# Seven SBUF buffers in one ring for output tiles, transposed w3 tiles and the remainders' gate products

## The chip, the core and the metric

The kernel runs on one core of one Trainium2 chip. The metric is the device time of one execution in microseconds. Before the change the median of three runs is 421.14 us (419.65 to 421.98). The engines are named as in the profile: PE is TensorE, with PEld for its weight loads, DVE is VectorE, ACT is ScalarE, POOL is GpSimd, and SP is SyncE, which here only issues transfers (DMAs).

## What is computed

An attention over 8 batches of 8 heads, whose queries are averaged in pairs, and then a feed-forward part with a product in place of an activation:

```
q_pool = q.reshape(B, H, S // 2, 2, D).mean(axis=3)          # 8, 8, 576, 64
attn = softmax(q_pool @ k.transpose / sqrt(D))               # keys: 1152
x = (attn @ v).transpose(0, 2, 1, 3).reshape(B * 576, H * D) # 4608 x 512
out = ((x @ w1) * (x @ w2) @ w3) @ w_out                     # w1, w2: 512 x 1024
```

Here w3 is 1024 x 1024 and w_out 1024 x 512. Output and inputs are float32; the kernel works in float16 with sums in float32.

## The kernel before

**Attention.** The heads are taken in 32 pairs P. POOL issues the loads of k, q and v (L110, L118, L125). The first pairs are transposed on PE, the later ones by transposing DMAs on SP (kT at L168, qT at L174). Scores are made in chunks of 512 columns for two heads (L296), in a PSUM tile `psc`; ACT takes the exponential into the ring `er` (L302). When a pair's scores are done, `attend` multiplies them with v (L315, L324) in bursts: 36 matmuls for each head into a PSUM bank `po`, plus 18 for the last 64 columns. DVE divides by the sums (L348, L351) and SP transposes the result into `xT` (L356). The last 64 of the 576 queries of a head, the remainders, go into `rems` (L362) and by transposes of their own (L335) into `xR`, which is copied across halves on DVE (L377).

**Feed-forward.** w3 @ w_out is multiplied once into `T16`: `w3_transpose` transposes a block of w3 on PE (L486), DVE copies it in two halves into a tile `w3T` (L477), and PE multiplies it with w_out (L498). For each batch, `gate` makes x @ w1 and x @ w2 into one PSUM bank (`pg`, L539). A copy of the first half goes to `asb` (DVE at L518; in the tail ACT at L515), and DVE multiplies both into the gate product `gT` (L531). `rows` multiplies `gT` with `T16` into a PSUM tile `pp` (L563). `store` evicts it, scaled, into a tile `osb` of 128 x 512 float32 (DVE at L553; in the tail ACT at L549), and `store_rows` has SP store that to the output (L629). The last tile is evicted in halves by `last_rows` (L640 on ACT, L643 on DVE; stores at L647).

The remainders of four batches form a unit of their own (`split=True`), once in the middle and once at the end. Its gate products are two tiles of 128 x 8 x 128 float16; they live until the unit's output rows are multiplied.

**Order.** The program is written out in Python with a manual schedule. A planner keeps one clock for each half of PE's rows (`clock`), times of DVE and of ACT, and two queues for each half: `prep` (transposes) and `ffn` (feed-forward blocks). It emits a chunk of scores when ACT will take it, a burst of `attend` when a pair is done, and otherwise the next feed-forward product (`step`). A block takes one of four PSUM banks with `take` and gives it back when its eviction is planned to end (`give`). So the order on each engine is fixed when the program is built; on the chip, each engine works its list in order, and semaphores hold an instruction until its operands and its buffer are there. `seen` and the loads of a pair five ahead follow each kT.

**Buffers.** A tile of the pool `ffp` has a tag; tiles of one tag share `bufs` buffers in turn. When a tile gets a buffer, its first writer waits for the last readers of the tile that had it. For an `osb` tile the last reader is its store. The tags that matter are `osb` with three buffers, and `w3T` with four, which the remainders' `gT` use too. All of these tiles have 2048 bytes in a partition. `w3T` tiles are written from 23.8 to 54.7 us, and no more than four of them are alive, which the planner takes care of (`len(w3T) < 4` at L765).

Of the kernel before, what the change touches and what calls it, by code (L numbers as in the profile page):

```python
# [7 lines left out]
FP32 = mybir.dt.float32  # L8
FP16 = mybir.dt.float16
# [14 lines left out]
def kernel(  # L24
# [13 lines left out]
    dm = H * D  # L38
# [3 lines left out]
    NF = dff // 128  # L42
# [9 lines left out]
    ffp = ctx.enter_context(tc.tile_pool(name="ffp", bufs=2))  # L52
# [33 lines left out]
    def vector(n, at):  # L86

        nonlocal vec
        vec = max(vec, at + T_SEM) + 0.16 + n / 960
        return vec  # L90

    def bank(pre, n, dt=FP32):
        if n >= 4:
            return psum.tile([128, 2, 512], FP32, tag="psc", bufs=2, name=pre)[:, 0, :]
        return psum.tile([128, 2048 // (4 if dt == FP32 else 2)], dt, tag=f"ff{n}", bufs=1,
                         name=pre)

    def take():
        return spare.pop(0)[1]
# [330 lines left out]
    w3T = {}  # L430
# [31 lines left out]
    def add(queue, block, cost, ready, emit):  # L462


        for h in block.tiles:
            for n in range(block.n_products):
                queue[h].append((block, n, cost, ready(n) if callable(ready) else ready, emit))

    def w3_transpose(c):

        w3T[c] = ffp.tile([128, NF, 128], FP16, tag="w3T", bufs=4, name="w3T")
        ready = [1e9]
        left = [2]
        landed = 13.0

        def out(t, at, h):
            nc.vector.tensor_copy(out=w3T[c][:, :, 64 * h:64 * h + 64],  # L477
                                  in_=t[:, 0:512].rearrange("p (a f) -> p a f", f=64))
            done = vector(256, at)
            left[0] -= 1  # L480
            if left[0] == 0:
                ready[0] = max(done + T_SEM, landed)
            return done

        def emit(t, s, n, start, stop):
            nc.tensor.transpose(t[:, 64 * n:64 * n + 64],  # L486
                                w3h[c // 2][s, c % 2, 128 * n:128 * n + 128], ident[s, s])
        for h in range(2):
            add(prep, Block("w3t", NF, (h,), lambda t, at, h=h: out(t, at, h), FP16),
                0.0285, [[0.0]], emit)  # L490

        def copy(t, at):
            nc.vector.tensor_copy(out=T16[:, c, :], in_=t)
            del w3T[c]
            return vector(512, at)

        def product(t, s, n, start, stop):
            nc.tensor.matmul(t, w3T[c][s, n, :], wosb[s, n, :], start=start, stop=stop,  # L498
                             skip_group_check=True)
        add(ffn, Block("pT", NF, (0, 1), copy), 0.216, [ready], product)  # L500

    def unit(x, places, ready, split=False, final=False):

        gT = {}
        gdone = [[[1e9] for _ in range(NF)] for _ in range(2)]
        n = 256

        def gate(ft, h):  # L510
            def mul(t, at):
                asb = ffp.tile([128, n], FP32, tag="asb", bufs=3, name="asb")
                b, a = t[:, n:2 * n], asb
                if tail:
                    nc.scalar.copy(out=a, in_=t[:, 0:n])  # L515
                    at += 0.4
                else:
                    nc.vector.tensor_copy(out=a, in_=t[:, 0:n])  # L518
                    vector(n, at)
                if h not in gT:  # L520
                    if split:
                        g = ffp.tile([128, NF, 128], FP16, tag="w3T", bufs=4, name="gT")
                        gT[h] = g.rearrange("p a f -> p (a f)").rearrange(
                            "p (a f) -> p a f", f=n)
                    else:
                        gT[h] = ffp.tile([128, NF, n], FP16, tag="g", bufs=4, name="gT")
                g = gT[h][:, ft % 4 if split else ft, 0:n]
                if not split:
                    g = g.rearrange("f (i p c) -> f i c p", p=64, c=2)
                    b, a = (y.rearrange("f (i c p) -> f i c p", c=2, p=64) for y in (b, a))  # L530
                nc.vector.tensor_mul(out=g, in0=b, in1=a)  # L531
                done = vector(n, at)
                gdone[h][ft][0] = done + T_SEM
                return done
            fs = slice(ft * 128, ft * 128 + 128)

            def emit(t, s, i, start, stop):
                w, m = divmod(i, H)
                nc.tensor.matmul(t[:, n * w:n * w + n], (w1sb, w2sb)[w][s, (m + h) % 2, m // 2, fs],  # L539
                                 x(h, s, m),  # L540
                                 start=start, stop=stop, skip_group_check=True)
            add(ffn, Block("pg", 2 * H, (h,), mul), 0.0025 + n / 2400,
                [ready, copied[2 * ft // NF]], emit)

        def rows(h, o, places):
            def store(t, at):
                osb = ffp.tile([128, dm], FP32, tag="osb", bufs=3, name="osb")
                if tail:
                    nc.scalar.activation(out=osb, in_=t, func=AF.Copy, bias=0.0,  # L549
                                         scale=1.0 / (SCL * SCL))  # L550
                    done = at + T_SEM + 0.65
                else:
                    nc.vector.tensor_scalar_mul(out=osb, in0=t, scalar1=1.0 / (SCL * SCL))  # L553
                    done = vector(512, at)
                store_rows(osb, places)
                return done
            cs = slice(o, o + 128)

            def g(s, i):
                return gT[i // 4][s, i % 4, cs] if split else gT[h][s, i, cs]  # L560

            def emit(t, s, i, start, stop):
                nc.tensor.matmul(t, g(s, i), T16[s, i, :], start=start, stop=stop,  # L563
                                 skip_group_check=True)
            if final:
                last.append((emit, store, places, lambda i: g(slice(0, 128), i)))
            else:
                add(ffn, Block("pp", NF, (0, 1), store), 0.216,
                    lambda i: [gdone[i // 4 if split else h][i]], emit)

        yield gate
        for h, o, to in places:
            rows(h, o, to)
# [43 lines left out]
    def rows_out(places, cols):  # L617

        (b0, c0), (b1, c1) = places
        if b0 == b1:  # L620
            rows = out[b0 * SQ:(b0 + 1) * SQ, cols].rearrange("(p c) m -> p c m", c=NJ)
            return [(slice(0, 128), rows[:, c0:c0 + 2])]
        return [(slice(64 * s, 64 * s + 64),
                 out[b * SQ:(b + 1) * SQ, cols].rearrange("(p c) m -> c p m", c=NJ)[c])
                for s, (b, c) in enumerate(places)]

    def store_rows(osb, places):
        for r, rows in rows_out(places, slice(0, dm)):
            nc.sync.dma_start(out=rows, in_=osb[r])  # L629

    def last_rows(places, lhsT):
        osb = ffp.tile([128, dm], FP32, tag="osb", bufs=3, name="osb")
        for h in range(2):
            hs = slice(256 * h, 256 * h + 256)
            pp = bank("pp", take())
            for ft in range(NF):
                nc.tensor.matmul(pp[:, hs], lhsT(ft), T16[:, ft, hs],  # L637
                                 start=(ft == 0), stop=(ft == NF - 1))
            if h == 0:
                nc.scalar.activation(out=osb[:, hs], in_=pp[:, hs], func=AF.Copy, bias=0.0,  # L640
                                     scale=1.0 / (SCL * SCL))
            else:
                nc.vector.tensor_scalar_mul(out=osb[:, hs], in0=pp[:, hs],  # L643
                                            scalar1=1.0 / (SCL * SCL))
            for s, (r, rows) in enumerate(rows_out(places, hs)):
                eng = nc.sync if s == 0 else nc.scalar
                eng.dma_start(out=rows, in_=osb[r, hs])  # L647
# [56 lines left out]
    c = 0  # L704
# [65 lines left out]
    for emit, store, _, _ in last[:-1]:  # L770
        n = take()
        t = bank("pp", n)
        for i in range(NF):
            emit(t, slice(0, 128), i, i == 0, i == NF - 1)
        give(n, store(t, clock[0]))
    last_rows(*last[-1][2:])


# [28 lines left out]
```

## Time and profile before

| what | us |
|---|---|
| median of three runs | 421.14 |
| the profiled execution | 418.11 |
| its span, from the first to the last instruction | 416.2 |
| evictions of `pp` by DVE (L553) | 26 of 0.69, from 118.9 to 347.3 |
| evictions by ACT (L549) | 9 of 0.60, from 375.8 to 410.7 |
| stores of `osb` by SP (L629) | 38, from 122.6 to 411.9 |
| a store from issue to landing, whole tiles | 4.0 (median) |

The granted TensorE clock was 1.00 throughout. One execution is profiled; its own time is its span and 1.9 us around it. A line of the profile's groups of instructions names the source line, the engine, the operation, what is written from what (`osb<-pp`), its count and its time. `[3.00 <-DMA x]` behind a line of the timeline is idle time of the engine before that instruction, and what ended it. An engine with the letter q (SPq) stands for issuing or waiting, not for work. The chain of work that ended last is followed back from the last instruction, at each step to what released it.

### The profile page before, as it was taken

What the parts mean: (1) busy time and instruction counts of PE and PEld (TensorE: products, weight loads), DVE (VectorE), ACT (ScalarE), POOL (GpSimd) and SP (SyncE); (2) the same over time, 40 slices, a digit from 0 to 9 for tenths busy, and PEclk for the clock granted to TensorE, in tenths of its full rate; (3) what the DMA queues carried; (4) which work ended last, traced back from release to release, by engine and by line L of the source; (5) the groups of instructions that cost most, each with busy time, mean ns of one, the idle gap of its engine ahead of it and who ended that gap; (6) DMA issues with size and microseconds to landing.
All of it is one profiled execution on the core that took longest, in us unless ns stands there. A gap on an engine that the chain in (4) does not pass through costs nothing.

```text
span 416.2 us, 16886 instructions
## 1 busy us (share of the span) xinstructions
PE 398.7 (96%) x7410; PEld 315.5 (76%) x7410; DVE 219.0 (53%) x586; ACT 323.5 (78%) x368; POOL 191.5 (46%) x209
## 2 busy tenths in 40 slices
PE   3699999999999999999999999899999999999996
PEld 1376775868769987987789886797789878987873
DVE  3256668765536644654466644365456645653530
ACT  3978889989889888778888987888887887854432
POOL 8244334870666676645656575566676400000000
PEclk9999999999999999999999999999999999999999
DMA  8999999999999998999999999999995155102004
GB/s 128 200 206 203 180 189 192 191 173 162 140 149 160 196 149 141 195 146 113 195 185 143 135 146 180 200 161 143 138 179 94 27 84 138 23 19 106 2 17 138
DMA packets 94217, 58.98 MB, mean 142 GB/s; under 512 B 64832, under 2 KB 84544, under 8 KB 94144
## 3 DMA queue, kind: packets, MB, share of 16 engines
q0 software_dynamic: 26528, 33.56, 53.1%
q1 hardware_dynamic: 67456, 24.22, 36.5%
q8 instruction: 58, 0.95, 1.0%
q10 hardware_dynamic: 160, 0.13, 0.1%
q14 instruction: 15, 0.12, 0.1%
HBM read 67.11 MB, written 9.44 MB: 184 GB/s over the span
## 4 chain that ended last, share of the span: by engine, by line
PE 91%; ACT 4%; DMA 2%; issue 1%; DVE 1%; POOL 0%; DVEq 0%; POOLq 0%
PE pg L539 29%; PE psc L296 19%; PE po L315 18%; PE pp L563 15%; PE pT L498 4%; ACT er L302 4%; PE po L324 3%; DMA out_dram<-osb 1%; PE t L264 1%; DMA kst<-in_k_dram 1%; PE sw L412 1%; PE w3t L486 1%; PE pp L637 0%; DVE osb L553 0%; PE tb L197 0%
## 5 line engine op out<-in xcount | busy, mean ns | idle before, releaser
L302 ACT ACTIVATE er<-psc 128x1024 f16<-128x1024 f32 x324 | 303.6, 1038 | 54.9 <-PE psc L296 54.8
L296 PE MATMUL psc<-qT,kT 64*128 64x512 f16 (+7 forms) x1152 | 130.0, 291 | 4.3 <-ACT er L302 3.9
L539 PE MATMUL pg<-xT,w2sb 64*128 64x256 f16 x1024 | 120.7, 269 | 0.1
L539 PE MATMUL pg<-xT,w1sb 64*128 64x256 f16 x1024 | 118.9, 269 | 1.0 <-issue 1.0
L539 PEld LDWEIGHTS <-w1sb 64*128 64x128 f16 x1152 | 90.4, 94 | 9.1 <-issue 1.3
L539 PEld LDWEIGHTS <-w2sb 64*128 64x128 f16 x1152 | 91.0, 94 | 6.4 <-issue 0.2
L563 PE MATMUL pp<-T,gT 64*128 64x512 f16 (+1 forms) x552 | 92.7, 376 | 0.0
L296 PEld LDWEIGHTS <-kT 64*128 64x128 f16 x1152 | 62.5, 95 | 31.6 <-issue 16.6
L315 PEld LDWEIGHTS <-er 128*128 128x128 f16 x2304 | 73.9, 98 | 13.5 <-issue 11.7
L315 PE MATMUL po<-vt,er 128*128 128x65 f16 x2304 | 80.3, 194 | 1.2 <-DVE osb L553 1.1
L531 DVE TENSOR_TENSOR gT<-pg,asb 128x256 f16<-128x256 f32 x144 | 64.2, 446 | 17.9 <-ACT asb L515 12.8
L518 DVE COPY asb<-pg 128x256 f32<-128x256 f32 x117 | 49.1, 420 | 34.5 <-PE pg L539 34.2
L348 DVE RECIPROCAL rz<-po 128x4 f32<-128x4 f32 x64 | 12.1, 189 | 82.0 <-PE po L315 43.7
L145 POOL TENSOR_TENSOR qp<-qst 64x1152 f16<-64x1152 f16 x23 | 54.5, 2368 | 1.0
L563 PEld LDWEIGHTS <-gT 64*128 64x128 f16 (+1 forms) x552 | 37.8, 94 | 17.2 <-issue 0.4
L170 POOL COPY seen<-kT 1x1 f16<-1x1 f16 x19 | 3.4, 181 | 80.9 <-DMA kT<-kc 80.9
L154 POOL COPY vt<-vst 128x1152 f16<-128x1152 f16 x28 | 32.1, 1150 | 3.9 <-issue 2.9
L125 POOL DMA_DIRECT2D vst<-in_v_dram x32 | 23.2, 725 | 17.1 <-DMA kst<-in_k_dram 6.1
L118 POOL DMA_DIRECT2D kst<-in_k_dram x33 | 24.0, 728 | 11.7 <-issue 3.0
L163 POOL COPY kc<-kst 128x1152 f16<-128x1152 f16 x23 | 26.8, 1163 | 5.7 <-DMA kT<-kc 5.7
L351 DVE TENSOR_TENSOR xn<-po,rz 128x256 f16<-128x256 f32 x64 | 27.2, 424 | 2.2
L498 PE MATMUL pT<-wosb,w3T 64*128 64x512 f16 x128 | 26.2, 377 | 0.0
(66 smaller groups left out, 238.1 us busy)
## 6 DMA issues: line engine op xcount, KB each, us to landing
qst<-in_q_dram POOLq DMA_DIRECT2D x32, 288.0 KB, 7.4
vst<-in_v_dram POOLq DMA_DIRECT2D x32, 288.0 KB, 9.0
kst<-in_k_dram POOLq DMA_DIRECT2D x31, 288.0 KB, 6.0
out_dram<-osb SPq DMA_DIRECT2D x32, 256.0 KB, 4.0
w3h<-in_moe_w_dram POOLq DMA_DIRECT2D x4, 512.0 KB, 15.2
wosb<-in_moe_w_out_dram POOLq DMA_DIRECT2D x1, 1024.0 KB, 13.7
xT<-xn SPq DMA_TRANSPOSE x64, 5.9
w1sb<-in_moe_w_dram POOLq DMA_DIRECT2D x2, 512.0 KB, 15.8
```

What stands on the lines that cost most here:

```text
L145: (eng or nc.vector).tensor_tensor(out=qps[pp][r].rearrange("p c u d -> p u c d"), in0=src[:, :, :, 0, :], in1=src[:, :, :, 1, :], op=ALU.add)
L154: (eng or nc.vector).tensor_copy(out=vts[P % 4][:, :, :, 0:D], in_=vst.pop(P))
L163: nc.gpsimd.tensor_copy(out=kc.rearrange("p j u d -> p u j d"), in_=kst.pop(P))
L296: nc.tensor.matmul(t[:, u, o:o + ln], kT[P][s, j, :], qv[s, f0:f0 + ln], start=True, stop=True)
L302: nc.scalar.activation(out=er[:, :, r:r + CH], in_=psc.pop(c), func=AF.Exp, bias=0.0, scale=SCALE)
L315: nc.tensor.matmul(po[:, VW * i:VW * i + D + 1], er[:, u, r:r + 128], vts[P % 4][:, u, j, 0:D + 1], start=(j == 0 and i == 0), stop=(j == ...
L351: nc.vector.tensor_tensor(out=xn, in0=acc[:, 0:4, 0:D], in1=rz[:, 0:4].to_broadcast([128, 4, D]), op=ALU.mult)
L498: nc.tensor.matmul(t, w3T[c][s, n, :], wosb[s, n, :], start=start, stop=stop, skip_group_check=True)
L518: nc.vector.tensor_copy(out=a, in_=t[:, 0:n])
L531: nc.vector.tensor_mul(out=g, in0=b, in1=a)
L539: nc.tensor.matmul(t[:, n * w:n * w + n], (w1sb, w2sb)[w][s, (m + h) % 2, m // 2, fs], x(h, s, m), start=start, stop=stop, skip_group_chec ...
L563: nc.tensor.matmul(t, g(s, i), T16[s, i, :], start=start, stop=stop, skip_group_check=True)
```

## The change

Two tags become one. The w3 tiles, the remainders' gate products and the output tiles share one ring of seven buffers, as many bytes as before:

```diff
     def w3_transpose(c):
-        w3T[c] = ffp.tile([128, NF, 128], FP16, tag="w3T", bufs=4, name="w3T")
+        w3T[c] = ffp.tile([128, NF, 128], FP16, tag="row", bufs=7, name="w3T")
...
                     if split:
-                        g = ffp.tile([128, NF, 128], FP16, tag="w3T", bufs=4, name="gT")
+                        g = ffp.tile([128, NF, 128], FP16, tag="row", bufs=7, name="gT")
...
             def store(t, at):
-                osb = ffp.tile([128, dm], FP32, tag="osb", bufs=3, name="osb")
+                osb = ffp.tile([128, dm], FP32, tag="row", bufs=7, name="osb")
...
     def last_rows(places, lhsT):
-        osb = ffp.tile([128, dm], FP32, tag="osb", bufs=3, name="osb")
+        osb = ffp.tile([128, dm], FP32, tag="row", bufs=7, name="osb")
```

The other gate products keep their own tag with four buffers. The planner's clocks, costs and limits are the same, and so is every call that emits an instruction.

## The prediction

> **What bounds the kernel now.** I read the page from the top: its first part for the engines, its fourth for the chain that ended last.
>
> ```profile
> span 416.2 us, 16886 instructions
> ...
> PE 398.7 (96%) x7410; PEld 315.5 (76%) x7410; DVE 219.0 (53%) x586; ACT 323.5 (78%) x368; POOL 191.5 (46%) x209
> ...
> PE 91%; ACT 4%; DMA 2%; issue 1%; DVE 1%; POOL 0%; DVEq 0%; POOLq 0%
> ```
>
> PE is busy for 96% of the span and holds 91% of the chain. So a changed wait on DVE, ACT or SP counts only as far as it makes PE pause. The same line of the chain has 2% for DMA; the chain by line puts 1% on `out_dram<-osb`, a store of an output tile. That does not belong on a chain in the middle of a kernel, so I asked for the waits around that tile.
>
> ```profile
> its engine sat idle before it (us, times) until:
>   PE pp L563: 17.8, 26
>   PE pp L637: 6.2, 2
>   DMA out_dram<-osb: 3.0, 1
> who waited for it (us, times):
>   DVE osb L553: 3.0, 1
>   PE po L315: 1.1, 1
> ...
> DMA to landing us min/median/max: 2.0/4.0/8.0
> ```
>
> Of all the evictions into osb tiles exactly one, with 3.0 us of idle time, waited for a store (for a buffer); the others waited for PE's product. One wait of PE, 1.1 us, was in turn for that eviction. The timeline of that stretch, first SP, then DVE, then PE:
>
> ```profile
> 259.07 3.60 SPq L356 DMA_TRANSPOSE xT<-xn  x2
> 262.76 1.18 SPq L335 DMA_TRANSPOSE wosb<-rems  x1
> 264.04 1.21 SPq L629 DMA_DIRECT2D out_dram<-osb  x2
> ```
> ```profile
> 259.32 0.69 DVE L553 TENSOR_SCALAR osb<-pp 128x512 f32<-128x512 f32 x1 [0.19 <-PE pp L563]
> ...
> 265.89 0.45 DVE L531 TENSOR_TENSOR gT<-pg,asb 128x256 f16<-128x256 f32 x1
> 269.34 0.69 DVE L553 TENSOR_SCALAR osb<-pp 128x512 f32<-128x512 f32 x1 [3.00 <-DMA out_dram<-osb]
> ```
> ```profile
> 267.72 1.27 PE L315 MATMUL po<-vt,er 128*128 128x65 f16 x36
> 270.08 1.25 PE L315 MATMUL po<-vt,er 128*128 128x65 f16 x36 [1.09 <-DVE osb L553]
> ```
>
> The tile written at 259.32 is full at 260.01. Its store is issued only at 264.04, since SP works in order and first issues three transposes (3.60 and 1.18 us). The store lands at 264.04 + 5.21 = 269.25 (5.21 is its piece in the chain). Three tiles later the ring of three is round: DVE is free at 265.89 + 0.45 = 266.34, the product was ready before that (DVE's wait for PE that the eviction carries ended at 265.83 by the semaphore's record), and it sits until 269.34. Its eviction frees the PSUM bank that the second half of an attention burst wants, so PE pauses 1.09 us.
>
> **The change, step by step.** I laid the instruction listings of the two programs side by side. On PE, DVE, ACT, POOL and SP every instruction, DMA issues included, stands in the same place; nothing is added, removed or moved. The planner's own rule (at most four w3T at once) is untouched. What differs is buffer addresses and the waits of DVE and ACT for a buffer. So the work is to take each eviction, find the new previous holder of its buffer, and read from the trace of before when that holder was done.
>
> 1. The one wait that goes. The osb tile at 269.34 no longer waits for the store issued at 264.04; in the new ring its buffer was last read by a store that landed at 259.44, and the product is ready at 265.83. So it starts behind the gate product at 266.36 or so, 3.0 us earlier, and ends at 267.05. Next late for PE is then nothing of this eviction: the second 36 matmuls of the burst can follow the first 36, which end at 268.99. PE saves 270.08 - 268.99 = **1.09 us**; the other 1.9 us of the wait were hidden under PE's gate matmuls and the first half of the burst.
>
> 2. The other 25 evictions on DVE and the 11 by ACT and DVE at the end (9 of L549, one each of L640 and L643). Before, all were ended by PE, so dropping waits for landed stores gains nothing. The tightest of these was the tile at 263.69, whose store had landed at 263.21, 0.48 us earlier. In the new ring the smallest margin between a buffer's release and its use is 5.0 us (the last tile: released 406.58, used 411.56). In the places where the new listing has a store's wait, it ended long ago.
>
> 3. Waits that are new. Two gate products of the last remainder batch (L531 at 394.78 and 397.06) now also wait for stores, of tiles that landed at 349.33 and 352.81: over 44 us early, cost nothing. If they were late, ACT's asb copies and the PE gate banks behind them would be, at up to the whole delay. The two copies to asb at 382.15 and 382.69 name an ACT instruction 8 us and more earlier: nothing. The w3T evictions (L477) keep exactly their waits. A queue instruction for an extra wait takes 21 ns on DVE (L553 has 19 of them, median 21 ns); a few go and come, none while PE waits: nothing, and bounded by 19 x 0.021 = 0.4 us either way.
>
> 4. Different addresses. No row shows an instruction whose time hangs on its buffer: the 26 evictions into three buffers take 676 to 693 ns. I take zero; the bound, were all 26 at the other end of that spread, is 0.4 us off the path.
>
> Does 1.09 us reach the end? Behind 270 the list of PE's waits has only this pause and one of 1.0 us for nothing that the profile shows; the stage from 272 to 363 has PE busy 90.02 of 91.00 us, and ACT, busy 76.13 there, has idle time in front of it at every burst to move along (3.19 us before 272.17, where the burst before had 2.01). DVE's copy of the remainders at 293.84 has the smallest margin to a transfer behind 270, 0.45 us. If that transfer did not come earlier too, DVE would wait 0.6 us; DVE's 3.0 us wait above showed that some 1.9 us can be hidden there, and I take the price as zero. The tail ends with matmuls and fixed stores and moves along.
>
> Sum, on the profiled execution (418.11 us, of which 416.2 span and 1.9 around it): 418.11 - 1.09 = 417.0. The median of the runs shown is 421.14, 3.0 above the profiled execution; no row says where those 3.0 go, and I leave them in both kernels: 421.14 - 1.1 = **420.0**.
>
> The trace's store took 5.21 us. The Trainium skill, DMA: Bandwidth & Descriptors, section Anatomy of one DMA, fits 2.0 us plus the bytes by 436 GB/s (it measured transfers issued by GpSimd; this one is SP's). For 256 KB that is an estimate of 2.6 us, the wait would be 0.3 us, PE would not pause, and the change would give nothing: that is the first rival below. This trace does not agree, with a median of 4.0 us; the measurement decides.
>
> **The rivals.**
>
> *No gain.* DVE's wait costs PE only what goes beyond 1.9 us, so the store has to land later than 264.04 + 4.1. This one took 5.2; the median of all is 4.0, the shortest 2.0. In an execution where it takes the median, PE does not pause even before the change, and the time stays 421.1. Against it: the stretch 264 to 272 moves 250 GB/s, the most of six stretches that I compared (157 in the long one before it, 109 behind), because a pair's loads of k, q and v (3 x 288 KB) are issued at 259.07 to 261.1, and they belong to the program, not to chance.
>
> *A larger gain.* The timed runs are 1.5 to 3.9 us longer than the profiled execution. If part of this is stores that land later, the old ring pays and the new one does not. At the largest landing time seen, 8.0 instead of 5.2, the pause is 1.1 + 2.8 = 3.9 us, and the time 417.2. The tile at 263.69, with a margin of 0.48, would be late too. For it: four evictions before the tail had margins of 0.5 to 2.1 us. Against it: in this profile all but one were met.
>
> *Slower: PE's instructions arrive late.* PE paused twice with no wait that the profile shows, 0.56 us before 180.91 (L324) and 0.98 us before 282.47 (L539). I read them as a late block of instructions: queue q8 brings 58 packets, 0.95 MB, some 16 KB each. The change moves all of PE behind 270 by 1.1 us against the transfers, so other blocks can be late. At 0.98 us each, one more cancels the gain; four more make 420.0 + 3.9 = 423.9. The point from which it is slower by 0.5% is (2.1 + 1.1) / 0.98 = 3.3 blocks. Against it: 2 of 58 were late in the whole span, and there are only some 25 behind 270. The Trainium skill, Runtime: NRT & Kernel Launch, section Instruction fetch mechanics, says that the fetch is mostly hidden; the two pauses are the exception here, if my reading of them is right.
>
> *The change doesn't do what it says.* If the pool handed out buffers so that a tile waits for a gate product still in use, time would be lost; the listing shows no such wait.
>
> **How the numbers follow.** Forecast, about 1 us off (0.3 to 2.1): 0.52, at 420.0. No gain, within 0.3 us or a little over: 0.15, at 421.1. Larger gain, over 2.1 us: 0.23, at 417.2. Slower rival: 0.10, at 423.9. That the change doesn't do what it says: under 0.01, and left out. The runs before spread 419.65 to 421.98, so under 0.5% (2.1 us) a measurement of this kernel can hardly be told from no change. Faster by over 0.5% is the larger gain, 0.23; slower by over 0.5% needs three to four late blocks, 0.08, and one or two of them leave it within; the rest, 0.69, is within 0.5%. The range goes from 417.4, just short of the largest store, to 421.9, where a median without gain could fall within the runs' spread (421.1 + 0.8); about 0.2 lies outside.
>
> **What would show it.** In the profile after, the waits around osb should have no row for `out_dram<-osb`; PE po L315 should have no wait for DVE osb L553; a burst of 72 should stand whole (2.3 us) near 267.7, and ACT's idle time at the next exponential fall from 3.19 to about 2.0. PE's busy time stays near 398.7 and the span falls to about 415.1. What would prove me wrong: a new wait of DVE or ACT for a store, more pauses of PE by "issue" (rival three), or timed runs that fall by far more than the one pause of the profile (rival two).

## The result, and the profile after

| | median us | runs |
|---|---|---|
| before, measured with the change | 420.23 (417.94 to 423.20) | 16 |
| after | 417.94 (414.81 to 419.83) | 16 |
| ratio after to before | 0.9951, 95% interval 0.9928 to 0.9973 | |

The change makes the kernel faster by 0.49%, which is 2.1 us of 420.2; the interval goes from 1.1 to 3.0 us. The forecast was 1.1 us, and 420.0 for a median that now measures 417.9, inside the range but near its lower end. Of the 2.1 us between these two, 0.9 is the median of before, which is 421.14 over three runs and 420.23 over 16; the rest is the gain.

The page of the kernel after:

```profile
span 416.9 us, 16877 instructions
...
PE 398.7 (96%) x7410; PEld 315.2 (76%) x7410; DVE 220.1 (53%) x586; ACT 323.6 (78%) x368; POOL 191.4 (46%) x209
...
PE 92%; ACT 4%; issue 1%; DMA 1%; DVE 1%; POOL 0%; DVEq 0%; POOLq 0%
```

PE is as busy as before to the tenth. DMA fell from 2% of the chain to 1%. Yet this span is not shorter but 0.7 us longer than the one of before; experiment 9 comes back to it. The waits around the output tiles in the kernel after:

```profile
its engine sat idle before it (us, times) until:
  PE pp L563: 17.4, 25
  PE pp L637: 6.2, 2
who waited for it (us, times):
```

The row for `out_dram<-osb` is gone, and nobody waits for an eviction. Then the place of the old pause, SP, DVE and PE of the kernel after:

```profile
263.66 1.19 SPq L335 DMA_TRANSPOSE wosb<-rems  x1
264.95 1.21 SPq L629 DMA_DIRECT2D out_dram<-osb  x2
```
```profile
265.77 0.45 DVE L531 TENSOR_TENSOR gT<-pg,asb 128x256 f16<-128x256 f32 x1
266.11 0.68 DVE L553 TENSOR_SCALAR osb<-pp 128x512 f32<-128x512 f32 x1
```
```profile
267.60 2.37 PE L315 MATMUL po<-vt,er 128*128 128x65 f16 x72
```

The tile that stood until 269.34 is evicted right behind the gate product, and the burst of 72 matmuls is whole. The store that it used to wait for is still late: issued at 264.95, and by its semaphore it landed at 271.73, 6.8 us later (5.2 in the first profile of before). By this landing, a ring of three would have held DVE some 2.5 us longer here than in the first profile of before.

### The profile page after: what moved, and what is told of

Read it like the earlier page. It is cut to its first block, busy times and chain, and to the rows that moved or that the text cites. A ratio compares the mean times of both kernels' runs of the same rounds, so it can differ in the third digit from the quotient of the medians.

```text
span 416.9 us, 16877 instructions
## 1 busy us (share of the span) xinstructions
PE 398.7 (96%) x7410; PEld 315.2 (76%) x7410; DVE 220.1 (53%) x586; ACT 323.6 (78%) x368; POOL 191.4 (46%) x209
## 4 chain that ended last, share of the span: by engine, by line
PE 92%; ACT 4%; issue 1%; DMA 1%; DVE 1%; POOL 0%; DVEq 0%; POOLq 0%
PE pg L539 29%; PE psc L296 18%; PE po L315 18%; PE pp L563 15%; PE pT L498 4%; ACT er L302 4%; PE po L324 3%; DMA kst<-in_k_dram 1%; PE t L264 1%; PE sw L412 1%; PE w3t L486 1%; PE pp L637 0%; DVE wosb L377 0%; PE tb L197 0%; POOL qst L110 0%
```

## The experiments

**Theory A**: the gain is the one wait of output tile 17 (counted from 0; the eviction at 269.34) for the store of tile 14; in most executions this store lands later than in the first profile, and so the pause is larger than 1.1 us. **Theory B**: several evictions wait for stores in the timed runs, and the gain is spread over them. **Theory C**: the new addresses matter, not the wait. Two more rivals, D and E, come up below.

### 1. One tile alone gets another buffer

```diff
-                osb = ffp.tile([128, dm], FP32, tag="osb", bufs=3, name="osb")
+                n, made[0] = made[0], made[0] + 1
+                if n == 17:
+                    osb = ffp.tile([128, dm], FP32, tag="w3T", bufs=4, name="osb")
+                else:
+                    osb = ffp.tile([128, dm], FP32, tag="osb", bufs=3, name="osb")
```

> The kernel before, in which the one output tile that waited (number 17 counted from 0, written at 269.3 us) takes a buffer of the ring of four w3 tiles, and nothing else is changed. Theory A, that the whole gain is this one wait: the same ratio to before as the changed kernel, 0.995 (0.993 to 0.997), and no eviction waits for a store around 266. Theory B, that the gain is spread over several evictions that only in the timed runs wait for a store (the tile at 263.7 had a margin of 0.5 us): less than half of it, 0.998 to 1.000. Theory C, that the new addresses matter and not the wait: 1.000.

Ratio to before 0.9955 (0.9931 to 0.9979). One tile of 36 in another buffer gives the gain of the whole change, which is theory A's figure. The profile also holds a wait at a later tile, which the first profile of before does not have; first that eviction on DVE, then the burst on PE:

```profile
310.46 0.69 DVE L557 TENSOR_SCALAR osb<-pp 128x512 f32<-128x512 f32 x1 [1.40 <-DMA out_dram<-osb]
```
```profile
268.67 2.37 PE L315 MATMUL po<-vt,er 128*128 128x65 f16 x72
```

At 310.46 tile 21 waits 1.40 us for a store, and no wait of PE follows from it: a wait under 1.9 us was hidden here too.

### 2. All tiles but that one

The same two branches, with the condition

```diff
-                if n == 17:
+                if n < 12 or 18 <= n < 30:
```

> The complement: tiles 0 to 11 and 18 to 29 take buffers of the ring of four, tiles 12 to 17 and the last ones keep the ring of three, so that the wait of tile 17 for the store of tile 14 stays, while nearly all other tiles have more room. Theory A: ratio 1.000 to before (0.998 to 1.002), DVE waits 3 to 6 us for a store at tile 17, and PE pauses 1 to 4 us there. Theory B: at least half of the gain, 0.997 or less.

Ratio 1.0003 (0.9978 to 1.0028): with that wait in place, more room for the others gives nothing. DVE, then PE:

```profile
270.55 0.69 DVE L557 TENSOR_SCALAR osb<-pp 128x512 f32<-128x512 f32 x1 [4.07 <-DMA out_dram<-osb]
```
```profile
267.85 1.27 PE L315 MATMUL po<-vt,er 128*128 128x65 f16 x36
271.29 1.25 PE L315 MATMUL po<-vt,er 128*128 128x65 f16 x36 [2.17 <-DVE osb L557]
```

DVE waits 4.07 us and PE pauses 2.17: the 1.9 us between the two are what PE had to do meanwhile, as in the first profile (3.00 and 1.09).

### 3 and 4. A ring of five, a ring of six

The changed kernel with another count in all four places:

```diff
-tag="row", bufs=7
+tag="row", bufs=5
```

> The changed kernel with a ring of five in place of seven. Two of the five hold the remainders' gate products while tiles 12 to 17 are written, which leaves three: by the listing, tile 17 waits for the store of tile 14 again. Theory A: ratio 1.000 to before, the pause of PE is back (1 to 4 us), though the addresses are again others and the other tiles have rings of five. Theory B: about 0.997. Theory C gives no reason why five should differ from seven: 0.995.

> The changed kernel with a ring of six. Tile 17 then waits for the store of tile 13, which landed at 263.2 in the profile of before, 2.6 us before it is needed (262.2 in the one after). Theory A: 0.995, as with seven, no wait for a store. If the stores of the timed runs are so late that even tile 13's is late (over 2.6 us later than in the profile), 0.997.

Five: 0.9992 (0.9964 to 1.0021). Six: 0.9944 (0.9918 to 0.9971). With five the wait is back; DVE, then PE of the ring of five:

```profile
269.83 0.69 DVE L553 TENSOR_SCALAR osb<-pp 128x512 f32<-128x512 f32 x1 [4.30 <-DMA out_dram<-osb]
```
```profile
270.58 1.43 PE L315 MATMUL po<-vt,er 128*128 128x65 f16 x36 [2.40 <-DVE osb L553]
```

The burst of the ring of six:

```profile
268.92 2.37 PE L315 MATMUL po<-vt,er 128*128 128x65 f16 x72
```

With six no eviction waits for a store, and the gain is there. So it is a threshold, in the number of buffers left while two hold the remainders' gate products: three are one too few, four are enough. The interval of the ring of five reaches down to theory B's 0.997, so there it is the pause in its profile that speaks for theory A. Theory C falls, since all rings from five to seven have new addresses, and with five the gain is gone. The ring of six costs 2048 bytes per partition less than the change, at the same time within the intervals.

### 5. The store that is late, issued by another engine

The kernel before, ring of three. One store of 38 goes out from ACT, so that it does not stand in SP's queue:

```diff
-                store_rows(osb, places)
+                store_rows(osb, places, nc.scalar if n == 14 else nc.sync)
```

> The kernel before with its ring of three, in which the store of tile 14 alone is issued by ACT and not by SP, so that it does not stand behind the transposes in SP's queue (4.0 us between the tile's end and the issue in the profile of before). Theory A, with the queue as the reason why the store is late: issued near 260.5 it lands near 265 to 266, tile 17 does not wait (or under 1.9 us), PE does not pause, ratio 0.995 to 0.998; ACT gives 0.6 us for the issue. Rival D, that the store is late for its flight alone, since the transfers are full between 259 and 270: it lands after 268 all the same, and the ratio is 1.000.

Ratio 0.9960 (0.9936 to 0.9985). ACT, then DVE (tiles 16 and 17), then PE:

```profile
262.12 0.67 ACTq L631 DMA_DIRECT2D out_dram<-osb  x1
```
```profile
267.09 0.69 DVE L554 TENSOR_SCALAR osb<-pp 128x512 f32<-128x512 f32 x1 [1.41 <-DMA out_dram<-osb]
268.77 0.68 DVE L554 TENSOR_SCALAR osb<-pp 128x512 f32<-128x512 f32 x1
```
```profile
270.25 2.37 PE L315 MATMUL po<-vt,er 128*128 128x65 f16 x72
```

The tile was full at 262.09, the store went out at once and landed at 267.77, before DVE was free; this whole stretch lies some 2 us later than in the first profile. Its flight was 5.7 us, no shorter than the others. So the transposes ahead of it in SP's queue (4.0 to 5.9 us from the tile's end to the issue in the three profiles of before) turn a slow store into a late one, and rival D falls: the flight alone would not have made PE pause. Tile 16 waited 1.41 us for another store; again no pause of PE.

### 6. Two buffers for output tiles in place of three

```diff
-                osb = ffp.tile([128, dm], FP32, tag="osb", bufs=3, name="osb")
+                osb = ffp.tile([128, dm], FP32, tag="osb", bufs=2, name="osb")
```

(and the same in `last_rows`).

> The kernel before with two osb buffers in place of three: the wait made larger and more frequent. By the landings in the profile of before, DVE waits at nine tiles before the tail: 0.9 and 1.6 us near 127, 5.6 at 166.7, 2.4 at 204, 0.1, 1.7, 5.6 and up to 4 from 259 to 270, 2.1 at 347. Theory A, with PE pausing by what goes beyond 1.9 us wherever a wait stands: 3.7 + 0.5 + 3.7 + 2 + 0.2, some 10 us, ratio 1.024 (1.015 to 1.035). If waits elsewhere are mostly hidden, 1.005 to 1.015.

Ratio 1.0228 (1.0170 to 1.0287), 9.6 us by 420, from only four runs; between the medians it is 7.9 us (427.88 and 419.96). The waits of the output tiles, then those of PE:

```profile
  DMA out_dram<-osb: 19.9, 9
```
```profile
PE pg L539 <- DVE osb L553: 5.9, 2, 5.3
PE po L315 <- DVE osb L553: 2.9, 2, 2.2
```

Of 19.9 us that evictions waited, PE lost 5.9 + 2.9 = 8.8. Each wait that cost anything, as a pair of DVE's wait and PE's pause: 2.12 and 0.53 near 131, 3.55 and 2.20 near 170, 7.44 and 5.35 near 272, 2.08 and 0.73 near 357. The hidden part is 1.35 to 2.1 us. The total was foreseen; the places less so: waits of 5.6 and up to 4 us were expected at tiles 16 and 17, and it was one of 7.44 at tile 16, behind which tile 17 waited for nothing. Of the nine waits seven lie before the tail, where nine were expected.

### 7 and 8. The kernel before, twice more

> The kernel before once more, for the size of the pause in another execution. Theory A, with stores that in most executions land later than in the first profile: DVE waits 3.5 to 6 us at tile 17 and PE pauses 1.6 to 4 us, always 1.9 us less than DVE. Otherwise 1.1 us as in the first profile, and the other 1 us of the gain is not in this pause.

> The same kernel a third time, with the same expectations as the second look: pause of PE 1.6 to 4 us, and 1.9 us less than DVE's wait.

The second profile of before, DVE and PE:

```profile
271.22 0.69 DVE L553 TENSOR_SCALAR osb<-pp 128x512 f32<-128x512 f32 x1 [4.62 <-DMA out_dram<-osb]
```
```profile
271.97 1.28 PE L315 MATMUL po<-vt,er 128*128 128x65 f16 x36 [2.72 <-DVE osb L553]
```

The third:

```profile
261.56 0.69 DVE L553 TENSOR_SCALAR osb<-pp 128x512 f32<-128x512 f32 x1 [0.71 <-DMA out_dram<-osb]
265.29 0.69 DVE L553 TENSOR_SCALAR osb<-pp 128x512 f32<-128x512 f32 x1 [2.27 <-DMA out_dram<-osb]
270.51 0.69 DVE L553 TENSOR_SCALAR osb<-pp 128x512 f32<-128x512 f32 x1 [3.72 <-DMA out_dram<-osb]
```
```profile
271.26 1.25 PE L315 MATMUL po<-vt,er 128*128 128x65 f16 x36 [2.10 <-DVE osb L553]
```

PE's pause in five executions that have the wait (three of before, experiments 2 and 3): 1.09, 2.72, 2.10, 2.17, 2.40, with a mean of 2.1 us. The first profile, on which the forecast was built, has the smallest of them. In the third, tiles 15 and 16 wait too, without a pause of their own; theory B had that much right, that such waits come and go, but they are hidden. There the difference between DVE's wait and PE's pause is 1.6 and not 1.9, probably because tile 16 was late already.

The pause is not all that the wait costs. The page of the second profile shows a granted TensorE clock below 0.9 in one of its 40 slices, just behind the pause, and the same kind of matmul takes longer there than ahead of the pause:

```profile
PEclk9999999999999999999999999989999999999999
```
```profile
266.57 0.27 PE L539 MATMUL pg<-xT,w2sb 64*128 64x256 f16 x1
274.64 0.42 PE L539 MATMUL pg<-xT,w2sb 64*128 64x256 f16 x1
```

The granted clock was 0.50 from 273.06 to 276.47, for 3.41 us. The profiles of experiments 2 and 3 have the same stretch behind their pauses of 2.17 and 2.40 us, and so has experiment 6 around the end of its pause of 5.35; the first and the third profile of before, with 1.09 and 2.10, have none. From the end of the pause to the 150th matmul behind it PE takes 6.87 us in these two, and 8.38, 8.50 and 8.37 with the lower clock (the second profile of before, experiments 2 and 3). So in three of the five, PE loses another 1.5 to 1.6 us.

The timed runs show it too, in the mean granted clock that each has. One such stretch takes 0.004 off the mean, and the fall at the very end that the profiles also have takes at most 0.002. Of the 52 runs of before that were measured with experiments 1 to 6, 27 have 0.996 or less. Of the 53 runs of the kernels without the old pause (after, experiments 1 and 5, the ring of six) not one has. Among the 35 runs of before that were measured with experiments 1 to 4, the median is 419.9 us for the 18 with the lower clock and 418.4 for the other 17; experiment 1 and the ring of six have 417.4 and 417.3. So there the gain is about 1.1 us over the runs without the lower clock, which is the forecast's figure, and 2.6 over those with it. With experiment 5 the two are 0.1 and 2.3 us. The runs with the lower clock may have the longer pauses too, so these differences are not the price of the clock alone.

### 9. The kernel after, once more

> The changed kernel once more, since its first profile has a span 0.7 us longer than that of before. Theory A: again no eviction waits for a store and PE does not pause near 268; what made the first profile long, a later start and 2.8 us of pauses for which the profile shows no wait, is of that execution. The three profiles of before have 1.5, 1.1 and 0.7 us of such pauses, so here 0.5 to 2 us, and a span of 414.3 to 416. Rival E, that the change moves PE against its supply of instructions for good: again 2 us or more of such pauses, at the same two places behind 270.

Span 415.9 us, no eviction waits for a store, and the burst is whole. The pauses for which no wait is shown sum to 1.0 + 0.6 + 0.5 = 2.1 us, at the edge of what was expected and of the rival's figure, but only one of them, of 0.46 us, lies behind 270. In the first profile of after they are 0.44, 1.25 and 1.06 us; the chain there shows one of them plainly:

```profile
267.66 2.30 PE po L315 x72
...
273.56 1.25 issue
274.81 0.70 PE pg L539 x9
```

Rival E may be partly right. Take PE's pauses behind 270 in ten profiles, all but that of experiment 6. Of the five with the old pause only the first of before has one by issue there (0.98 us before 282.47), the other four none. Of the five without it four have one near 274 to 276 (1.25, 0.46, 0.24, 0.12 us), and experiment 1 has none there. Over the whole span behind 60 us such pauses (over 0.15 us) sum to 0.4 to 1.5 us in the five with the old pause and to 1.3 to 2.8 us in the five without. Much of that must be chance, since in experiments 1 and 5 all of it lies before 216 us, where they run as the kernel before does. A second small thing shows only without the old pause: PE waits 0.1 to 0.9 us near 295 in all five, as here in the second profile of after, PE and then DVE:

```profile
294.84 0.80 PE L563 MATMUL pp<-T,gT 64*128 64x512 f16 x5 [0.41 <-DVE handed L455]
```
```profile
294.02 0.59 DVE L377 COPY wosb<-wosb 64x512 f16<-64x512 f16 x2 [1.21 <-DMA wosb<-rems]
```

DVE's copy of the remainders waits for its transpose, and the copy for the next half of a product stands behind it. It is so in experiment 5 and with the ring of six too. In the first profile of after and in experiment 1 the copy starts without a wait, but the two together take 1.46 and 1.56 us and not 0.59; why is not shown. So part of what PE saves near 268 is given back within 30 us, by a few tenths at each place.

## Why the prediction was right, and where it was short

*The waits* were right. From the listing and the trace of before, one eviction of 37 would lose a wait and none would get one. Experiments 1 and 2 part the change into this tile and all the rest: 0.9955 and 1.0003.

*The cover of 1.9 us* was right at this place: 1.91, 1.90, 1.90 and 1.90 us in four profiles, 1.6 in a fifth with three waits in a row. With two buffers it is 1.35 to 2.1.

*The pause of 1.09 us* is the term that was mis-sized. It was read from one execution, the one of five with the shortest pause; in the five it is 2.1 in the mean. The interval of the timed runs, 1.1 to 3.0 us, reaches down to the forecast's figure, so it is the repeated profiles that tell.

*The clock* is a term that the sum lacks. Behind the longer pauses PE loses another 1.5 to 1.6 us at half the granted clock, in three of the five profiles and, by their mean clock, in 27 of 52 runs of before. That the mean pause equals the 2.1 us of the timed runs is therefore a coincidence: the clock comes on top, and against both stand 0.1 to 0.9 us near 295 and pauses by issue. The ten profiles taken alone would hardly have shown the gain: their spans have a mean of 417.2 us with the old pause and of 416.6 without.

*The 3.0 us* between the median and the profiled execution were left in both kernels. Against that, the second profile of before (420.28 us, pause 2.72) is 2.2 us longer than the first (418.11, pause 1.09): 1.6 for the pause and 1.5 for the clock, less the 0.98 us pause by issue that only the first has behind 270. The third (418.41, pause 2.10), without the lower clock and without that pause by issue, is 0.3 us longer than the first.

*The rival of a larger gain* had the right mechanism, stores that land later, and nearly the right point: the gain is 2.1 us, just where that case began and the forecast's own ended. It too priced the pause alone and not the clock. Its other leg, the tile at 263.69, does wait at times (2.27 us in the third profile of before), but hidden.

*The rival of no gain* asked for a landing within 4.1 us of 264.04. None of the five profiles with the wait had it: the store flew 4.6 to 6.1 us there, issued between 264.0 and 265.8. The median of 4.0 over all stores was the wrong row for this place, as the prediction suspected from the 250 GB/s there. The bytes alone do not order the flights, though: in the profile after, 264 to 272 moves 184 GB/s, and the store flew 6.8 us. The estimate of 2.6 us from the fit in the Trainium skill, DMA: Bandwidth & Descriptors, section Anatomy of one DMA, is further off still in this stretch.

*What was to be seen after*: a whole burst near 267.7 (267.60), no wait for a store, and ACT's idle time falling from 3.19 to about 2.0 (1.93) all came. The span of 415.1 did not: 416.9, and 415.9 in the second profile. For the first profile the sum over PE's path is: 1.09 us saved; 0.49 lost at the start, where PE's first matmul came at 6.64 and not 6.15 us; 1.2 lost in pauses by issue (2.75 us and not 1.54); 0.1 behind the remainders' copy. That is +0.7, the difference that the spans show. The start is 6.26 in the second profile, and 6.11 to 6.30 in the three of before, so it varies between executions of one kernel.

*DVE's copy of the remainders*, priced at zero, does cost: PE pauses 0.1 to 0.4 us near 295 in the profiles of after, of experiment 1 and of the ring of six, and 0.9 in experiment 5. DVE waits 1.2 to 1.7 us there in three of these profiles, where the prediction foresaw at most 0.6.

What stays open: whether the pause near 274 to 276 comes with the change for good or by chance. It was not taken away by an experiment, and at some 0.5 us it is within the interval of any timed run. Open too is how the 2.1 us divide between the pause and the clock, since no run has the one without the chance of the other, and why the store flies longer in this stretch.

## What to carry to other kernels

A tile that waits for its buffer costs what the bound engine loses, and that is the wait less the work in hand (here some 1.9 us), and whatever the engine's clock does behind the pause (here up to 1.6 us more). Before pricing such a wait from one profile, take a second and a third: when the late thing is a transfer, the one figure can be half the usual (here 1.09 and a mean of 2.1). And a ring is sized by the place where most of its tiles live at once: here the output tiles had three buffers where four were needed, sharing supplied the fourth, and 6 buffers in all did what 7 do.

## What the runs showed of the hardware

The granted TensorE clock fell to 0.50 for 3.41 us at or behind a pause of PE of 2.17, 2.40, 2.72 and 5.35 us, and not behind those of 1.09, 2.10 and 2.20 (the last in experiment 6, near 171). So the length of the pause alone does not decide. In all four profiles the fall came 249.17 us after the clock's first record, which is 73 times 3.413 us; so it looks as if the clock were set in steps of 3.41 us, and as if it mattered how a pause lies between two of them. That is read from the traces and was not tried.

PE's pauses with no wait shown end soon after a packet of 16 KB on the instruction queue q8 has landed: in 19 of 22 such pauses (over 0.08 us, behind 60 us, in ten profiles) PE goes on 1.3 to 1.6 us after one. With 58 packets in 416 us, one in some 7 us, chance would give about one of 22. So they do look like late blocks of instructions, as the prediction read them: 0.1 to 1.3 us each, one to four in a profile. No experiment took the late blocks away. They come and go between executions of one kernel, and make single spans a poor measure of a change of one or two microseconds. The Trainium skill, Runtime: NRT & Kernel Launch, section Instruction fetch mechanics, says that the cost of a block's boundary is mostly hidden; these runs agree for most of the 58 blocks, and, if the pauses are late blocks, put a price on the others.
